# Transposing the first block of x with the DMA crossbar instead of TensorE in a fused two-layer MLP

## The chip, the cores and the metric

The kernel runs on one core of one Trainium2 chip. Times are device microseconds (us) of one execution; medians come from three to eleven executions. A profiled execution has a span, from the first to the last instruction of the program, some 1.8 us shorter than its time (292.11 us had a span of 290.3).

## The reference, cut to what matters

```python
B, S, D, F = 1, 2048, 576, 4608          # x [S, D], w1 [D, F], w2 [F, D], all bf16
h = jnp.einsum("bsd,df->bsf", x, w1) + b1
r = jnp.where(h > zero, h, zero)
h = r * r
out = jnp.einsum("bsf,fd->bsd", h, w2) + b2
```

## The kernel before: the parts that matter

x is worked off in four blocks of 512 rows. The first layer needs x transposed (D on partitions). Blocks 1 to 3 are transposed by the DMA crossbar (`dma_start_transpose`); block 0, which the first matmuls wait for, by TensorE through PSUM. D is 4.5 times 128: four full K tiles (`O` to `O+3`) and a strip. `w1n` holds the first 512 columns of w1 in natural K tiles of 128 ("full matmuls", L194); the other 4,096 columns are in `w1_h`, half of them on partitions 0 to 63 and half on 64 to 127, and are worked off by pairs of 64-row matmuls that run side by side ("row-tiled matmuls", 16 row groups j of 18 matmuls). `w1_h` comes in chunk pairs of one or two row groups: (0,1), (1,2), (2,4) and so on.

```python
WARM = [512] * 6 + [256]
for i, n in enumerate(WARM):             # warm-up of TensorE on constants
    keep(nc.tensor.matmul(wps[:, 0:n], lhsT=ones[:, 0:P], rhs=ones[:, 0:n], start=True, stop=True))
...
load_x(nc.sync, 0); load_x(nc.scalar, 1); load_x(nc.sync, 2); load_x(nc.scalar, 3)   # four lines
for k in range(NK):
    load_w1n(nc.sync, k)
...
for j in range(RT):                      # block 0: 20 TensorE transposes
    ...
    for i in range(3):
        keep(nc.tensor.transpose(ta[:, i, :], xs[:, j, i * P:(i + 1) * P], ident[:]))
    keep(nc.vector.tensor_copy(out=xT0[:, O:O + 3, cols], in_=ta[:, :, :]))
    ...
dup_windows(0)                           # two DVE copies, lower half to upper and back
...
for (j0, j1) in [(0, 1), (1, 2), (2, 4), (4, 6), (6, 8), (8, 10), (10, 12)]:
    load_w1(nc.sync, 0, j0, j1)
    load_w1(nc.sync, 1, j0, j1)
load_xT(1)                               # crossbar transposes of block 1
for (j0, j1) in [(12, 14), (14, 16)]:
    load_w1(nc.sync, 0, j0, j1)
    load_w1(nc.sync, 1, j0, j1)
...
a_full(0, "k_outer")                     # 16 full matmuls, 4 for the strip
a_rows(0, 12, 1)                         # row-tiled matmuls; copies of block 1 at row group 12
```

## Time and profile before

| | |
|---|---|
| time, median of the first three runs | 292.98 us |
| span of the profiled run | 290.3 us |
| TensorE busy | 285.7 us, 98% |
| first full matmul | 5.71 us |
| first row-tiled matmul | 9.75 us |
| w1 pair of row groups 12 and 13 complete | 31.13 us, first used at 33.08 |
| first second-layer matmul | 75.90 us |

The page of the kernel before, its lines of busy time and of the chain that ended last (shares by engine):

```profile
PE 285.7 (98%) x2409; PEld 178.0 (61%) x2412; DVE 81.5 (28%) x189; ACT 94.2 (32%) x154; POOL 2.7 (1%) x10
...
PE 98%; ACT 0%; issue 0%; DVE 0%
```

TensorE does everything, and whatever does not make it wait costs nothing. Its waits, in total over the run (who waited for what: us, times, longest):

```profile
PE wps L61 <- PEq L306: 0.8, 1, 0.8
PE pn L194 <- ACT xTw L143: 0.4, 1, 0.4
PE pn L194 <- issue: 0.3, 2, 0.2
```

So there is 0.4 us to be had from waiting, and the time before the first full matmul. TensorE's timeline in the head (start us, us, engine, line, operation, tiles; in brackets the idle time before it and what ended that):

```profile
0.78 2.93 PE L61 MATMUL wps<-const-bfloat16-1.0 128*128 128x512 bf16 x7 [0.78 <-PEq L306]
...
5.71 1.89 PE L194 MATMUL pn<-xTw,w1n 128*128 128x512 bf16 x8 [0.43 <-ACT xTw L143]
...
9.75 0.38 PE L173 MATMUL ph<-xTw,w_h 64*128 64x512 bf16 x1
```

Warm-up to 3.7 us, transposes between, full matmuls from 5.71, row-tiled ones from 9.75. The SP queue in the same run (the time is from the first issue of a group to the end of the last):

```profile
0.74 0.85 SPq L70 DMA_DIRECT2D x_sb<-in_x_dram  x2
1.65 1.85 SPq L73 DMA_DIRECT2D w1n<-in_w_dram  x4
3.61 13.67 SPq L80 DMA_DIRECT2D w_h<-in_w_dram  x14
17.32 6.75 SPq L120 DMA_TRANSPOSE xTw<-in_x_dram  x1
```

w1 is issued from 3.61 us on, and then the DMA engines have a backlog. The second half of the pair for row groups 12 and 13, looked at alone (its issue on SP, and its time to landing):

```profile
L80 SPq DMA_DIRECT2D w_h<-in_w_dram x1: 638/638/638, 26.1 to 26.1; - x1
...
DMA to landing us min/median/max: 5.1/5.1/5.1
```

It lands at 31.13 us. Row group 12 starts at 33.06 us and needs it at 33.08: **1.95 us to spare**.

### The profile page before, as it was taken

What the parts mean: (1) busy time and instruction counts of PE and PEld (TensorE: products, weight loads), DVE (VectorE), ACT (ScalarE), POOL (GpSimd) and SP (SyncE); (2) the same over time, 40 slices, a digit from 0 to 9 for tenths busy, and PEclk for the clock granted to TensorE, in tenths of its full rate; (3) what the DMA queues carried; (4) which work ended last, traced back from release to release, by engine and by line L of the source; (5) the groups of instructions that cost most, each with busy time, mean ns of one, the idle gap of its engine ahead of it and who ended that gap; (6) DMA issues with size and microseconds to landing.
All of it is one profiled execution on the core that took longest, in us unless ns stands there. A gap on an engine that the chain in (4) does not pass through costs nothing.

```text
span 290.3 us, 5455 instructions
## 1 busy us (share of the span) xinstructions
PE 285.7 (98%) x2409; PEld 178.0 (61%) x2412; DVE 81.5 (28%) x189; ACT 94.2 (32%) x154; POOL 2.7 (1%) x10
## 2 busy tenths in 40 slices
PE   8999999999999999999999999999999999999995
PEld 4444444444677777777744444444447777777774
DVE  3344544444531011110025444444440111100111
ACT  4566666666400000000027666666670000000000
POOL 3000000000000000000000000000000000000000
PEclk9999999999999999999999999999999999999999
DMA  7999999900000000000000000000000000000000
GB/s 203 214 212 177 255 357 265 164 1 2 0 23 0 23 20 20 23 3 20 20 23 0 3 0 2 0 2 0 2 0 2 20 24 20 21 2 23 20 20 24
DMA packets 27096, 16.05 MB, mean 55 GB/s; under 512 B 11028, under 2 KB 27040, under 8 KB 27072
## 3 DMA queue, kind: packets, MB, share of 16 engines
q1 hardware_dynamic: 26688, 15.32, 23.9%
q8 instruction: 19, 0.31, 0.4%
q10 hardware_dynamic: 288, 0.30, 0.3%
q0 software_dynamic: 96, 0.07, 0.1%
q14 instruction: 5, 0.04, 0.0%
HBM read 11.36 MB, written 2.36 MB: 47 GB/s over the span
## 4 chain that ended last, share of the span: by engine, by line
PE 98%; ACT 0%; issue 0%; DVE 0%
PE po L233 49%; PE ph L173 42%; PE pn L194 5%; PE wps L61 1%; PE ph L175 1%; PE pn L188 1%; PE ta L138 0%; ACT xTw L143 0%; DVE o_sb L242 0%; ACT xTw L144 0%; PE tb L141 0%; PE tb L142 0%; PE b1T_ps L151 0%; PE pn L190 0%
## 5 line engine op out<-in xcount | busy, mean ns | idle before, releaser
L233 PE MATMUL po<-w_sb,hT 128*128 128x288 bf16 x1152 | 141.4, 286 | 0.0
L233 PEld LDWEIGHTS <-hT 128*128 128x128 bf16 x1152 | 112.7, 98 | 28.8
L173 PE MATMUL ph<-xTw,w_h 64*128 64x512 bf16 x576 | 124.6, 376 | 0.0
L175 PE MATMUL ph<-xTw,w_h 64*128 64x512 bf16 x576 | 124.6, 376 | 0.0
L173 PEld LDWEIGHTS <-w_h 64*128 64x128 bf16 x576 | 54.1, 94 | 68.3
L161 ACT ACTIVATE r<-ph,b1T 128x512 bf16<-128x512 f32 x128 | 81.1, 685 | 41.6 <-PE ph L175 41.6
L162 DVE TENSOR_TENSOR hT<-r 128x512 bf16<-128x512 bf16 x144 | 61.2, 426 | 77.3 <-ACT r L161 76.7
L175 PEld LDWEIGHTS <-w_h 64*128 64x128 bf16 x576 | 54.1, 94 | 0.0
L242 DVE TENSOR_TENSOR o_sb<-po,b_bc 128x288 bf16<-128x288 f32 x32 | 13.3, 453 | 123.9 <-PE po L233 123.9
L161 ACT ACTIVATE r<-pn,b1T 128x512 bf16<-128x512 f32 x16 | 10.3, 688 | 78.8 <-PE pn L190 77.5
L194 PE MATMUL pn<-xTw,w1n 128*128 128x512 bf16 x61 | 14.0, 379 | 0.8 <-ACT xTw L143 0.4
L194 PEld LDWEIGHTS <-w1n 128*128 128x128 bf16 x64 | 6.0, 98 | 8.0 <-issue 1.4
L61 PE MATMUL wps<-const-bfloat16-1.0 128*128 128x512 bf16 (+1 forms) x7 | 2.9, 594 | 0.8 <-PEq L306 0.8
L113 DVE COPY xTw<-xTw 64x2048 bf16<-64x2048 bf16 x4 | 2.8, 690 | 0.4 <-ACT xTw L144 0.3
L114 DVE COPY xTw<-xTw 64x2048 bf16<-64x2048 bf16 x4 | 2.7, 687 | 0.1
L139 DVE COPY xTw<-ta 128x384 bf16<-128x384 bf16 x4 | 1.3, 358 | 4.2 <-PE ta L138 4.2
L188 PE MATMUL pn<-xTw,w1n_89 64*128 64x512 bf16 x8 | 2.4, 379 | 0.0
L190 PE MATMUL pn<-xTw,w1n_89 64*128 64x512 bf16 x8 | 2.4, 379 | 0.0
L61 PEld LDWEIGHTS <-const-bfloat16-1.0 128*128 128x128 bf16 x7 | 0.9, 135 | 2.1 <-issue 2.1
L98 ACT ACT_TABLE_LOAD x1 | 1.3, 1283 | 1.7 <-PEq L306 1.7
L138 PE MATMUL ta<-ident,x_sb 128*128 128x128 bf16 x12 | 1.6, 265 | 0.0
L143 ACT COPY xTw<-tb 128x128 bf16<-128x128 bf16 x4 | 1.1, 282 | 1.2 <-PE tb L142 1.1
(21 smaller groups left out, 10.2 us busy)
## 6 DMA issues: line engine op xcount, KB each, us to landing
w_sb<-in_w_dram SPq DMA_DIRECT2D x6, 864.0 KB, 11.4
w_h<-in_w_dram SPq DMA_DIRECT2D x14, 288.0 KB, 7.4
out_dram<-o_sb SPq DMA_DIRECT2D x15, 144.0 KB, 1.8
w_h<-in_w_dram SPq DMA_DIRECT2D x4, 144.0 KB, 4.1
w1n<-in_w_dram SPq DMA_DIRECT2D x4, 128.0 KB, 4.0
x_sb<-in_x_dram ACTq DMA_DIRECT2D x2, 144.0 KB, 3.0
x_sb<-in_x_dram SPq DMA_DIRECT2D x2, 144.0 KB, 2.8
b_bc<-in_b_dram SPq DMA_DIRECT2D x1, 144.0 KB, 7.6
```

Source lines behind the costliest of these rows:

```text
L61: keep(nc.tensor.matmul(wps[:, 0:n], lhsT=ones[:, 0:P], rhs=ones[:, 0:n], start=True, stop=True))
L113: keep(nc.vector.tensor_copy(out=xT[0:H, SPC:SPC + 4, :], in_=xT[H:P, E3:E3 + 4, :]))
L114: keep(nc.vector.tensor_copy(out=xT[H:P, SPC:SPC + 4, :], in_=xT[0:H, O:O + 4, :]))
L161: keep(nc.scalar.activation(out=r[:], in_=bank[:], func=ACT.Relu, bias=b1T[:, ft:ft + 1], scale=1.0))
L162: keep(nc.vector.tensor_tensor(out=hTs[sb][:, ft, :], in0=r[:], in1=r[:], op=ALU.mult))
L173: keep(nc.tensor.matmul(bx[:], lhsT=w1_h[0:H, LO_C[i], jc], rhs=xT[0:H, LO_W[i], :], start=(i == 0), stop=(i == NC - 1)))
L175: keep(nc.tensor.matmul(by[:], lhsT=w1_h[H:P, UP_C[i], jc], rhs=xT[H:P, UP_W[i], :], start=(i == 0), stop=(i == NC - 1)))
L188: keep(nc.tensor.matmul(banks[2 * i][:], lhsT=w1n8[0:H, i, :], rhs=xT[0:H, SPC, :], start=start, stop=stop))
L190: keep(nc.tensor.matmul(banks[2 * i + 1][:], lhsT=w1n8[H:P, i, :], rhs=xT[H:P, E3, :], start=start, stop=stop))
L194: keep(nc.tensor.matmul(banks[g][:], lhsT=w1n[:, k, g * P:(g + 1) * P], rhs=xT[:, O + k, :], start=start, stop=stop))
L233: keep(nc.tensor.matmul(po[h][:, 0:DH], lhsT=hT[:, ft, jj * P:(jj + 1) * P], rhs=w2_sb[:, ft, h * DH:(h + 1) * DH], start=(i == 0), stop=( ...
L242: keep(nc.vector.tensor_tensor(out=o_sb[:, h * DH:(h + 1) * DH], in0=po[h][:, 0:DH], in1=b2_bc[:, h * DH:(h + 1) * DH], op=ALU.add,))
```

## The change

The intent: free TensorE of 20 transposes and ACT and DVE of 12 evictions, and start the full matmuls on the first 256 rows while the second 256 are still on their way. The w1n loads move to the ScalarE queue, so that they need not queue behind the transposes.

```diff
-    WARM = [512] * 6 + [256]
+    WARM = [512] * 8
...
-    load_x(nc.sync, 0)
-    load_x(nc.scalar, 1)
-    load_x(nc.sync, 2)
-    load_x(nc.scalar, 3)
+    for h in range(2):
+        rc = slice(h * SB // 2, (h + 1) * SB // 2)
+        keep(nc.sync.dma_start_transpose(out=xT_blk[0][:, O:O + NK, rc], in_=x2[rc, 0:P * NK]))
+    keep(nc.sync.dma_start_transpose(out=xT_blk[0][:, E3:E3 + 1, :], in_=x2[0:SB, D - P:D]))
     for k in range(NK):
-        load_w1n(nc.sync, k)
+        load_w1n(nc.scalar, k)
+    load_w1(nc.scalar, 0, 0, 1)
+    load_w1(nc.scalar, 1, 0, 1)
...   (the TensorE transposes of block 0 and their evictions go)
-                for k in range(NK):
-                    for g in range(G):
-                        full(g, k, k == 0, False)
+                for h in range(2):
+                    hc = slice(h * SB // 2, (h + 1) * SB // 2)
+                    for k in range(NK):
+                        for g in range(G):
+                            keep(nc.tensor.matmul(banks[g][:, hc], lhsT=w1n[:, k, g * P:(g + 1) * P],
+                                                  rhs=xT[:, O + k, hc], start=(h == 0 and k == 0), stop=False, ...))
...
-    for (j0, j1) in [(0, 1), (1, 2), (2, 4), (4, 6), (6, 8), (8, 10), (10, 12)]:
+    for (j0, j1) in [(1, 2), (2, 4), (4, 6), (6, 8), (8, 10), (10, 12)]:
```

More of the change, by code (lines that the diff above doesn't have):

```diff
@@ L58 @@
     ones = nc.const_aps.tensor(1.0, [P, 512], BF16)
-    WARM = [512] * 6 + [256]
+    WARM = [512] * 8
     for i, n in enumerate(WARM):
         keep(nc.tensor.matmul(wps[:, 0:n], lhsT=ones[:, 0:P], rhs=ones[:, 0:n], start=True, stop=True))
-    xs = const.tile([P, RT, D], BF16, name="x_sb")
     w1n = wpool.tile([P, NK, GW], BF16, name="w1n")
@@ L67 @@
     w1_v = w1.rearrange("(c p) f -> p c f", p=H)
-    def load_x(eng, rt):
-        keep(eng.dma_start(out=xs[:, rt, :], in_=x2[rt * P:(rt + 1) * P, :]))
     def load_w1n(eng, k):
@@ L81, in load_w1, with alloc_xT @@
                       in_=w1_v[:, :, GW + h * FH + j0 * P:GW + h * FH + j1 * P]))
-    load_x(nc.sync, 0)
-    load_x(nc.scalar, 1)
-    load_x(nc.sync, 2)
-    load_x(nc.scalar, 3)
+    E3, O, SPC, E = 0, 1, 5, 6
+    xT_blk = {}
+    def alloc_xT(sb):
+        xT_blk[sb] = xtpool.tile([P, NC, SB], BF16, name="xTw", tag="xTw")
+    alloc_xT(0)
+    for h in range(2):
+        rc = slice(h * SB // 2, (h + 1) * SB // 2)
+        keep(nc.sync.dma_start_transpose(out=xT_blk[0][:, O:O + NK, rc], in_=x2[rc, 0:P * NK]))
+    keep(nc.sync.dma_start_transpose(out=xT_blk[0][:, E3:E3 + 1, :], in_=x2[0:SB, D - P:D]))
     for k in range(NK):
-        load_w1n(nc.sync, k)
+        load_w1n(nc.scalar, k)
+    load_w1(nc.scalar, 0, 0, 1)
+    load_w1(nc.scalar, 1, 0, 1)
     ident = const.tile([P, P], BF16, name="ident")
@@ L98 @@
     keep(nc.scalar.activation(out=warm[:], in_=nc.const_aps.tensor(0.0, [P, 1], FP32), func=ACT.Relu))
-    E3, O, SPC, E = 0, 1, 5, 6
     LO_W = [O, O + 1, O + 2, O + 3, E, E + 1, E + 2, E3, SPC]
@@ L104 @@
     UP_C = [1, 3, 5, 7, 8, 2, 4, 6, 0]
-    xT_blk = {}
-    def alloc_xT(sb):
-        xT_blk[sb] = xtpool.tile([P, NC, SB], BF16, name="xTw", tag="xTw")
     def dup_windows(sb):
@@ L130 @@
     b2_bc = const.tile([P, D], BF16, name="b2_bc")
-    alloc_xT(0)
-    xT0 = xT_blk[0]
-    for j in range(RT):
-        cols = slice(j * P, (j + 1) * P)
-        ta = ps_h.tile([P, 3, P], BF16, name="ta", tag="ph")
-        for i in range(3):
-            keep(nc.tensor.transpose(ta[:, i, :], xs[:, j, i * P:(i + 1) * P], ident[:]))
-        keep(nc.vector.tensor_copy(out=xT0[:, O:O + 3, cols], in_=ta[:, :, :]))
-        tb = ps_o.tile([P, 2, P], BF16, name="tb", tag="po")
-        keep(nc.tensor.transpose(tb[:, 0, :], xs[:, j, 3 * P:4 * P], ident[:]))
-        keep(nc.tensor.transpose(tb[:, 1, :], xs[:, j, D - P:D], ident[:]))
-        keep(nc.scalar.copy(out=xT0[:, O + 3, cols], in_=tb[:, 0, :]))
-        keep(nc.scalar.copy(out=xT0[:, E3, cols], in_=tb[:, 1, :]))
     dup_windows(0)
@@ L188, in pair @@
             keep(nc.tensor.matmul(banks[2 * i][:], lhsT=w1n8[0:H, i, :], rhs=xT[0:H, SPC, :],
-                             start=start, stop=stop))
+                             start=start, stop=stop, skip_group_check=order == "k_outer"))
             keep(nc.tensor.matmul(banks[2 * i + 1][:], lhsT=w1n8[H:P, i, :], rhs=xT[H:P, E3, :],
-                             start=start, stop=stop))
+                             start=start, stop=stop, skip_group_check=order == "k_outer"))
         def full(g, k, start, stop):
@@ L205, in a_full @@
             if order == "k_outer":
-                for k in range(NK):
-                    for g in range(G):
-                        full(g, k, k == 0, False)
-                    if k == 1:
-                        make_b1T()
+                for h in range(2):
[3 more added lines that the diff above has]
+                            keep(nc.tensor.matmul(banks[g][:, hc], lhsT=w1n[:, k, g * P:(g + 1) * P],
+                                                  rhs=xT[:, O + k, hc], start=(h == 0 and k == 0), stop=False,
+                                                  skip_group_check=True))
+                        if h == 1 and k == 0:
+                            make_b1T()
             else:
```

## The prediction

> **What bounds the kernel.** TensorE. The chain of waits puts 98% of the 290.3 us span on PE. By stage windows PE is busy 65.1 of 65.25 us (9.75 to 75) and 71.95 of 72.0 (75 to 147); the change touches none of that. Only the head can move. In the timeline warm-up matmuls run 0.78 to 3.71 us, block 0's PE transposes 3.5 to 5.3, the first real matmul starts at 5.71, the row-tiled matmuls at 9.75.
>
> **What it removes.** 20 PE transposes and 12 evictions (DVE 358 ns, ACT about 280 ns). On PE's chain they cost 2.0 us (3.71 to 5.71), but w1n loads meanwhile (lands at 4.9 to 7.3 us), so 1 to 1.5 us at most is on offer.
>
> **What it adds.**
> - Three crossbar transposes on SP. The unobstructed 512x512 one of the trace (issued at 52.5 us) took 2.22 us on SP and 6.6 us to landing; the 512x128 ones 1.25 us on SP, 3.0 to 4.6 us to landing. Estimate for a 256-row half alone: 1.2 us to the first packet, 2 us of packets, 1.4 us to the semaphore, so landing at 5.3 us.
> - Contention. The w1n loads and the first w1 pair (0.8 MB) run on the ScalarE queue beside the transposes. The Trainium skill (DMA: Bandwidth & Descriptors, "Queues, rings and completion order") says that DMA engines take queues in turn, packet by packet (no trace here shows this mix); 1 KB packets beside 256 B ones would take most of the rate until about 5 us. Estimates: first half lands at 6.2 (5.3 to 7.3), second at 7.4, last strip at 8.
> - PE: 32 matmuls of 256 columns for 16 of 512, the same array time (16 x 0.216 = 3.46 us), unless weight loads (98 ns) stop hiding behind 110 ns matmuls: up to 0.3 us. The warm-up ends at 4.2 us instead of 3.7.
>
> **On the critical path.** First real matmul at 6.2 instead of 5.71; 3.6 us of full matmuls to 9.8; the pairs need the strip and one window copy (8 + 0.69): no extra wait. Row-tiled matmuls start at about 10.4 instead of 9.75: +0.65 us. Later w1 chunks: the last two pairs landed 2.0 and 1.4 us ahead of use (31.1 for 33.1, 35.5 for 37). The transposes delay that queue by an estimated 1 to 2 us, PE is itself 0.65 late: 0 to 0.5 us of stall. Sum: +0.8 us.
>
> **Prediction: 293.8 us, range 292.4 to 296.2.** Faster by over 2%: 0.005; within 2%: 0.975; slower by over 2%: 0.02.
>
> **What shows each step.** Timeline: first full matmul between 5.5 and 7.3 us; PE idle about 2 us after the warm-up, released by the transpose's DMA, not by w1n; 32 matmuls about 110 ns apart; row-tiled start 9.9 to 11.5; landings as above; later stage windows unchanged but for small waits on w1 before 38 us.
>
> **What would make it wrong.** (a) The first half lands before 4.7: a gain of up to 1 us. (b) Contention doubles the transposes' time: +2 to 3 us. (c) The idle gap closes the clock gate. The skill (TensorE: Matmul & The Clock Gate, Part 1) gives a window of 3.4 us (here matmuls went from 427 to 216 ns at about 4.5 us, which fits). A 2 us gap should be survived; if not, add 1.5 to 2 us. (d) w1 chunks slip beyond their slack: +1 to 2 us around 33 to 38 us.

## More of the kernel before

One execution was abnormal: the profiled run of the kernel called dead_L took 1,734 us, with TensorE six times as slow as ever (one row group of matmuls took 11.9 us where 1.94 is usual). It is left out of all times. Only its early DMA records are used, and that is said where it is done.

## The result, and the profile after

The median went from 292.80 us (4 runs, 292.60 to 293.26) to 296.52 us (4 runs, 296.03 to 296.91). The ratio is 1.0124, 95% interval 1.0103 to 1.0144. All ratios in this text are the mean time of one kernel's fast runs over that of the other's fast runs of the same rounds, so not quite the ratio of the medians quoted. Slower by 1.2% counts as "the same" at 2%, but it is far outside the noise, and outside the predicted range (292.4 to 296.2). The profiled run of before (292.11 us) is faster than each of its four, and that of after (296.91) is the slowest of its four, so the spans differ by 4.8 us.

The same lines of the page after; the chain now holds DMA and SP:

```profile
PE 286.8 (97%) x2409; PEld 178.0 (60%) x2409; DVE 80.2 (27%) x185; ACT 92.5 (31%) x146; POOL 2.7 (1%) x10
...
PE 86%; SPq 8%; DMA 4%; issue 0%; DVE 0%
```

TensorE's waits after. There are now three kinds of data to wait for, x, w1n and w1:

```profile
PE pn L196 <- DMA xTw<-in_x_dram: 1.8, 2, 1.0
PE pn L196 <- DMA w1n<-in_w_dram: 1.1, 1, 1.1
PE ph L161 <- DMA w_h<-in_w_dram: 1.1, 1, 1.1
PE wps L61 <- PEq L296: 0.8, 1, 0.8
```

TensorE's timeline in the head, after:

```profile
0.78 3.57 PE L61 MATMUL wps<-const-bfloat16-1.0 128*128 128x512 bf16 x8 [0.78 <-PEq L296]
5.36 1.71 PE L196 MATMUL pn<-xTw,w1n 128*128 128x256 bf16 x12 [1.01 <-DMA xTw<-in_x_dram]
8.17 0.61 PE L196 MATMUL pn<-xTw,w1n 128*128 128x256 bf16 x4 [1.09 <-DMA w1n<-in_w_dram]
9.61 0.60 PE L196 MATMUL pn<-xTw,w1n 128*128 128x256 bf16 x4 [0.82 <-DMA xTw<-in_x_dram]
...
11.94 0.38 PE L159 MATMUL ph<-xTw,w_h 64*128 64x512 bf16 x1
```

The first full matmul comes 0.35 us *earlier* than before. Then the last w1n tile is waited for until 8.17 us and the second row half until 9.61, and the row-tiled matmuls start at 11.94 us, 2.19 us late. Two short waits for the first and the third w1 pair follow, seen at TensorE's weight loads (PEld):

```profile
12.44 0.09 PEld L161 LDWEIGHTS <-w_h 64*128 64x128 bf16 x1 [0.61 <-DMA w_h<-in_w_dram]
16.59 0.09 PEld L161 LDWEIGHTS <-w_h 64*128 64x128 bf16 x1 [0.58 <-DMA w_h<-in_w_dram]
```

With them TensorE is 2.96 us late from row group 3 on (by the start of the second of each pair of matmuls). The crossbar transposes of block 0 on SP (ns on SP, min/median/max, and the time from issue to landing):

```profile
L88 SPq DMA_TRANSPOSE xTw<-in_x_dram x2: 1286/1304/1322, 0.7 to 2.1; - x2
L89 SPq DMA_TRANSPOSE xTw<-in_x_dram x1: 1254/1254/1254, 3.5 to 3.5; - x1
...
DMA to landing us min/median/max: 4.6/7.1/7.4
```

The first half took 4.6 us (landed at 5.32), as estimated for one alone. The second took 7.4 (9.56 us) and the strip 7.1 (10.61). The next place where time goes is at row group 12, in TensorE's timeline:

```profile
36.11 0.39 PE L159 MATMUL ph<-xTw,w_h 64*128 64x512 bf16 x1
37.58 0.39 PE L161 MATMUL ph<-xTw,w_h 64*128 64x512 bf16 x1 [1.08 <-DMA w_h<-in_w_dram]
```

The pair of row groups 12 and 13, complete at 31.13 us before, is complete at 37.53 now: its second half was issued late and then took no longer than before:

```profile
L76 SPq DMA_DIRECT2D w_h<-in_w_dram x1: 634/634/634, 32.7 to 32.7; - x1
...
DMA to landing us min/median/max: 4.8/4.8/4.8
```

From 40 us on nothing differs (TensorE is busy 35.00 of the 35 us from 40 to 75), and the first second-layer matmul starts at 80.42 us instead of 75.90: +4.52 us.

### The profile page after: what moved, and what is told of

The parts are those of the page before. It is cut to its first block, busy times and chain, and to the rows that moved or that the text cites. A ratio compares the mean times of both kernels' runs of the same rounds, so it can differ in the third digit from the quotient of the medians.

```text
span 295.1 us, 5438 instructions
## 1 busy us (share of the span) xinstructions
PE 286.8 (97%) x2409; PEld 178.0 (60%) x2409; DVE 80.2 (27%) x185; ACT 92.5 (31%) x146; POOL 2.7 (1%) x10
## 4 chain that ended last, share of the span: by engine, by line
PE 86%; SPq 8%; DMA 4%; issue 0%; DVE 0%
PE po L223 48%; PE ph L159 21%; PE ph L161 13%; SPq L76 5%; PE pn L180 4%; SPq L119 3%; DMA xTw<-in_x_dram 3%; DMA w_h<-in_w_dram 2%; SPq L88 0%; SPq L120 0%; PE pn L174 0%; DVE o_sb L232 0%; PE pn L176 0%
## 5 line engine op out<-in xcount | busy, mean ns | idle before, releaser
L180 PE MATMUL pn<-xTw,w1n 128*128 128x512 bf16 x48 | 10.9, 379 | 0.0
L180 PEld LDWEIGHTS <-w1n 128*128 128x128 bf16 x48 | 4.5, 98 | 5.9 <-issue 0.8
L196 PE MATMUL pn<-xTw,w1n 128*128 128x256 bf16 x32 | 4.2, 273 | 3.0 <-DMA xTw<-in_x_dram 1.8
L196 PEld LDWEIGHTS <-w1n 128*128 128x128 bf16 x32 | 3.0, 99 | 4.8 <-issue 2.8
L61 PE MATMUL wps<-const-bfloat16-1.0 128*128 128x512 bf16 x8 | 3.6, 628 | 0.8 <-PEq L296 0.8
L73 POOL DMA_DIRECT2D w1n_89<-in_w_dram x2 | 1.2, 629 | 0.0
```

What stands on the lines that cost most here:

```text
L180: keep(nc.tensor.matmul(banks[g][:], lhsT=w1n[:, k, g * P:(g + 1) * P], rhs=xT[:, O + k, :], start=start, stop=stop))
L196: keep(nc.tensor.matmul(banks[g][:, hc], lhsT=w1n[:, k, g * P:(g + 1) * P], rhs=xT[:, O + k, hc], start=(h == 0 and k == 0), stop=False, s ...
```

## The experiments

Fourteen kernels ran; all gave correct results. Theory A, to begin with: the transposes make the whole early DMA stream late, above all w1. Its rivals: B, only the late head counts; C, SP is held back by waits for completions; D, the halves and 256-column matmuls cost; E, the second queue costs by itself. Theories on the clock (H), on a drain per transpose (P) and on DMA engines in step (L) came up on the way.

### The queue change alone (q_only)

```diff
 # against before
-    load_x(nc.scalar, 1)            # and row tile 3 likewise
+    load_x(nc.sync, 1)
-        load_w1n(nc.sync, k)
+        load_w1n(nc.scalar, k)
```

> Kernel before with the queue part alone: all four x loads on SP, the four w1n loads on the ScalarE queue, TensorE transposes kept, no crossbar transpose of block 0. Theory A (the crossbar transposes beside the w1n loads move too few bytes per us, so the whole w1 stream comes late): no loss, 0.998 to 1.003 of before, first w1 chunks landing within 1 us of before's (8.5 and 9.95 us), packets of 256 B about 20 ns. Rival E (two hardware queues at once are what slows the start): at least +1.5 us and packets of w1 slow (over 28 ns) here too.

Measured: 296.33 us, ratio 1.0117, against 292.37 for before: as slow as the whole change, and not what I expected. In the profiled run (293.86 us) w1 was on time (first chunk at 7.84 us, 7.75 before), so neither A nor E as I had put it holds. The loss there is in the head: with w1n on its own queue its bytes arrive beside x and not behind it, and with all of x on SP the last x load is issued at 2.13 us and not at 1.18 (the edit does both). The last x tile landed at 6.50 us (4.36 before), and the first full matmul came at 7.43 us. The three timed runs were another 2.3 to 2.9 us slower (296.18 to 296.79), and they have a mean granted TensorE clock of 0.994 where the profiled run has 1.0: 0.6% of 294 us is 1.7 us lost, one stretch of 3.4 us at half clock (the profile of w1n_pairs, below, has such a stretch). So there was a third cause to look at, the clock gate; it covers 1.7 of the 2.3 to 2.9 us.

### Filling the gaps of that kernel (q_warm)

```diff
 # against q_only
+        if j >= 1:
+            for _ in range(3):
+                keep(nc.tensor.matmul(wps[:, 0:512], lhsT=ones[:, 0:P], rhs=ones[:, 0:512], start=True, stop=True))
         ta = ps_h.tile([P, 3, P], BF16, name="ta", tag="ph")
```

> q_only with three more 512-column warm-up matmuls ahead of each of the last three row tiles' transposes, which fill TensorE's waits for x. In three of four runs of q_only the mean granted clock was 0.994 (1.7 us lost) at 294.3 to 295.0 us of span, in the fourth 1.0 at 292.1. Theory H (the gaps of 0.4 to 0.6 us in the head make the clock gate close once more for one window): all four runs at 0.998 to 1.0, median 293 to 294.5. Rival E (the two queues are slow by themselves, the clock is a bystander): the median stays near 296.

Measured: 294.44 us, ratio 1.0066, clock 0.999 to 1.0 in all four runs. Theory H holds: with the gaps filled by useless matmuls the gate stayed open and 1.9 us came back. What stays over before (1.8 us) is the late x: first row-tiled matmul at 11.70 us, +1.94. For the kernel after itself the gate is not the cause as far as its profile shows: the clock opened at 4.33 us, as early as in before (4.52), and stayed open until TensorE was done, and this run was the slowest of the four. The mean clock of its other runs (0.998 to 1.0) says less: the profiles of one_queue and w1_first have a mean of 1.0 too, though their clock opened only at 12.18 and 9.18 us. The records begin at the first opening, so 0.994 points to a later closing (what closed at the end of a profiled run cost 0.002 at most), but 1.0 does not show an early opening.

### Transposes that nobody reads (dead_T), and plain loads that nobody reads (dead_L)

```diff
 # against before, behind the w1n loads on SP
+    dead = const.tile([P, 5, SB], BF16, name="dead")
+    for h in range(2):
+        rc = slice(h * SB // 2, (h + 1) * SB // 2)
+        keep(nc.sync.dma_start_transpose(out=dead[:, 1:1 + NK, rc], in_=x2[rc, 0:P * NK]))
+    keep(nc.sync.dma_start_transpose(out=dead[:, 0:1, :], in_=x2[0:SB, D - P:D]))
 # dead_L instead:
+    dead = const.tile([P, RT, D], BF16, name="dead")
+    for rt in range(RT):
+        keep(nc.sync.dma_start(out=dead[:, rt, :], in_=x2[rt * P:(rt + 1) * P, :]))
```

> Kernel before plus the same three crossbar transposes into a tile that nobody reads, on SP behind the w1n loads; TensorE's own head is untouched, so the first full matmul stays near 5.7 us and the first row-tiled one near 9.8 to 10.5. Theory A: the w1 stream comes 3 us or more late and TensorE stalls on w1 before 40 us: +1.5 to +4 us though no matmul reads the transposes. Rival B (only the wait of the head for the transposes costs): within 0.7 us of before.

> Kernel before plus four plain loads of block 0 of x (576 KB) into a tile nobody reads, at the place where dead_T had its three transposes. Theory A with the transposes as the cause: the plain loads delay the w1 stream by only 1.6 to 2.2 us (dead_T: 3.7 us at the first chunk and 4.6 at the third pair), so +0 to +1.2 us in time against +3.9 for dead_T. Rival (any extra 0.6 MB at that place costs this): +3 us or more.

Measured: dead_T 296.28 us, ratio 1.0127; dead_L 293.71 us (its three normal runs), ratio 1.0041 (interval 1.0024 to 1.0058). TensorE's waits in dead_T:

```profile
PE ph L180 <- DMA w_h<-in_w_dram: 1.2, 2, 0.9
PE ph L178 <- DMA w_h<-in_w_dram: 1.0, 1, 1.0
```

No matmul reads these transposes, and yet they cost 3.7 us by the ratio, nearly all of it at waits on w1, and all of it before row group 4: from there on TensorE is 3.80 us late, and row group 12 adds nothing. (The first full matmul is 0.46 us later, but so is that of before_w1, whose head is that of before. In these two profiles the clock opened at 6.46 and 5.87 us, and in before at 4.52: a single profile's head can differ by this much.) This is against rival B and for theory A, that w1 comes late. The same data as plain loads costs 1.2 us. In the landings, the third w1 pair's first half came at 11.34 us before, 13.62 with the plain loads (from the abnormal execution's DMA records, where w1 does not depend on TensorE) and 15.93 with the transposes. So at that place the three transposes delay the stream by 4.6 us, the plain loads by 2.3.

A rival: that SP takes long to issue transposes. The SP queue in dead_T, and then in dead_L (early records of the abnormal execution):

```profile
3.64 3.02 SPq L92 DMA_TRANSPOSE dead<-in_x_dram  x2
6.71 1.26 SPq L93 DMA_TRANSPOSE dead<-in_x_dram  x1
8.01 13.98 SPq L80 DMA_DIRECT2D w_h<-in_w_dram  x14
```

```profile
3.68 1.75 SPq L91 DMA_DIRECT2D dead<-in_x_dram  x4
5.48 14.58 SPq L80 DMA_DIRECT2D w_h<-in_w_dram  x14
```

The first w1 load is issued 4.40 us later than in before (3.61 us) and 1.87 us later: nearly all of the 4.6 and most of the 2.3. Meanwhile the DMA engines ran short of work in dead_T (from 9 to 10 us; the last two figures are their busy share and GB/s):

```profile
9.00:10.00 1.00, 1.00 (x7) 0.34 (x7) 0.00 (x0) 0.00 (x0) 0.00 (x0) 1.00 0.29 67
```

So what dead_T shows is the time that transposes take on SP. In the kernel after it is another matter: there SP issued its first w1 load (of the second pair) at 4.76 us, not later than in before (5.05), and the DMA engines were busier and moved less. From 2 to 13 us in before, then in after:

```profile
2.00:13.00 11.00, 10.57 (x78) 5.31 (x78) 4.82 (x12) 5.95 (x16) 1.38 (x3) 1.00 1.08 244
2.00:13.00 11.00, 7.88 (x50) 4.19 (x50) 1.57 (x3) 2.02 (x3) 1.39 (x3) 1.00 1.27 180
```

This agrees with theory A as it stands in q_only's expectation (too few bytes per us), but no experiment isolates it.

### Everything on one queue (one_queue), with a longer warm-up (one_queue_warm), with one transpose (one_queue_ns)

```diff
 # one_queue, against after
+    for k in range(NK):
+        load_w1n(nc.sync, k)            # ahead of the transposes
     for h in range(2):
         ...
-    for k in range(NK):
-        load_w1n(nc.scalar, k)
-    load_w1(nc.scalar, 0, 0, 1)         # the first w1 pair goes back to SP too
-    load_w1(nc.scalar, 1, 0, 1)
 # one_queue_warm, against one_queue
-    WARM = [512] * 8
+    WARM = [512] * 16
 # one_queue_ns: one_queue with one 512-row transpose and 512-column matmuls
```

> Kernel after with everything of the head on SP, w1n first, then the three transposes, then w1. Theory A with mixing as the cause: the transposes, now with no other hardware queue beside them, land within 4.5 us of their issue each (after: 3.2, 7.4 and 7.2 us), w1 packets stay near 20 ns and 47 ns, loss under 2 us. If instead the transposes slow the DMA engines by themselves: w1 chunks late by 3 us or more as in after, loss 3 to 4 us, one queue or two.

> one_queue with 16 warm-up matmuls in place of 8, which fill TensorE's wait until the first half lands at 7.0 us. Theory H (in the profile of one_queue the clock opened at 12.2 us only, and three timed runs have 0.994, because the wait of 2.7 us falls into the gate's window): the clock opens before 8 us and stays open, no run at 0.994, time 1.2 to 2.6 us less than one_queue, 292.8 to 294.2. Rival (the clock is a bystander): within 0.5 us of one_queue.

> one_queue with a single 512-row transpose (and 512-column matmuls) in place of the two halves. Theory P (each transpose has a drain of about 1 us in which the DMA engines move little, so a third transpose instruction costs the stream about 1 us): the transposes' last strip and the first w1 chunk land 0.6 to 1.2 us earlier than in one_queue (8.6 and 9.9 us), time 0.5 to 1.5 us less than one_queue. Rival D (the 256-column matmuls are what costs): strip and w1 chunk land as in one_queue, within 0.3 us, and only matmul times change.

Measured: one_queue 295.36 us (ratio 1.0105), one_queue_warm 294.98 (1.0080), one_queue_ns 297.97 (1.0178). In one_queue the three transposes landed 4.4, 4.1 and 3.2 us after their issue (7.4 and 7.1 for the last two in after), which points to the traffic beside them as what stretched them in after (their order and time of issue changed as well). But the loss is 3.1 us by the ratio, not under 2 as expected: they are issued later here, so is w1 (first load at 6.78 us, behind the transposes on SP, and not at 3.61), the first matmul starts at 7.06 us, and its wait of 2.71 us went with a clock gate that stayed shut: by the clock records of the trace it opened at 12.18 us only. The three timed runs (0.994) point to a closing after the opening. With 16 warm-up matmuls the clock opened at 4.66 us, no run was below 1.0, and the row-tiled matmuls started at 11.14 us instead of 13.63. That is 2.5 us won in the head; the time fell by only 0.4 us (0.7 by the ratios), because TensorE now waited for w1 (0.97 us at 16 us) and row groups 12 and 13 were late as well. The single transpose, expected to win about 1 us, took 6.4 us to land and lost 2.6 (part of it to the clock: three timed runs have 0.988 or 0.994): theory P falls, at least as I had put it.

### The halves (no_split), and the same with a longer warm-up (no_split_warm)

```diff
 # no_split, against after
-    for h in range(2):
-        rc = slice(h * SB // 2, (h + 1) * SB // 2)
-        keep(nc.sync.dma_start_transpose(out=xT_blk[0][:, O:O + NK, rc], in_=x2[rc, 0:P * NK]))
+    keep(nc.sync.dma_start_transpose(out=xT_blk[0][:, O:O + NK, :], in_=x2[0:SB, 0:P * NK]))
     ...  (and the 512-column matmuls of before)
 # no_split_warm, against no_split
-    WARM = [512] * 8
+    WARM = [512] * 16
```

> Kernel after without the row halves: one 512-row transpose and matmuls of 512 columns. Theory A: the w1 stream is as late as in after (chunk of rows 12 and 13 lands at 36 to 38 us), so the total is within 0.7 us of after although the first full matmul starts later (8 to 10 us instead of 5.4). Rival D (the halves and the 256-column matmuls cost the time): faster than after by 1 us or more. Rival B (the late start of the head alone sets the loss): slower than after by 1 us or more, as the first matmul starts later.

> no_split with 16 warm-up matmuls in place of 8, which fill the wait until the 512 rows land at 6.7 us. Theory H: the first 8 full matmuls take 1.9 us and not 3.2 as in no_split, the row-tiled start comes 0.8 to 1.4 us earlier (10.7 to 11.3 us), time 0.8 to 1.6 us less than no_split, unless the w1 stream now ends the stall (chunk of rows 12 and 13 landed at 34.6 us there, with 0.9 us to spare). Rival: within 0.4 us of no_split.

Measured: no_split 294.93 us, ratio 1.0092; no_split_warm 295.18 us, ratio 1.0090. By the ratios no_split is 0.9 us better than after, between what A and D had expected, and the intervals overlap; D is not settled by the time. The traces show that 256-column matmuls are not what costs (in after, twelve of them took 1.47 us), but all 512 rows together landed at 6.68 us here, and in after the second half alone at 9.56. In one_queue it was the other way round. Whether halves help depends on what runs beside them, and I can't say how.

The pair shows better than any other how a gain is given back. TensorE's first full matmuls in no_split, and then in no_split_warm:

```profile
6.73 3.23 PE L178 MATMUL pn<-xTw,w1n 128*128 128x512 bf16 x8 [2.37 <-DMA xTw<-in_x_dram]
```

```profile
6.74 1.89 PE L178 MATMUL pn<-xTw,w1n 128*128 128x512 bf16 x8
```

The longer warm-up did what it should: the clock is open, eight matmuls take 1.89 us and not 3.23, and the row-tiled start comes 1.0 us earlier (11.13 us). Yet the time is the same. TensorE's waits in no_split_warm show where it went:

```profile
PE ph L159 <- DMA w_h<-in_w_dram: 0.8, 1, 0.8
```

This wait is at 35.7 us, row group 12 again. In no_split no matmul waited for w1.

### Where w1 is issued from (w1_sp, w1n_pairs), and in which order (w1_first)

```diff
 # w1_sp, against after: the first w1 pair back on SP, behind the transposes
-    load_w1(nc.scalar, 0, 0, 1)
-    load_w1(nc.scalar, 1, 0, 1)
 # w1n_pairs, against after: two w1n loads of 256 KB
-    for k in range(NK):
-        load_w1n(nc.scalar, k)
+    for k in (0, 2):
+        keep(nc.scalar.dma_start(out=w1n[:, k:k + 2, :],
+                                 in_=w1[k * P:(k + 2) * P, 0:GW].rearrange("(k p) f -> p k f", p=P)))
 # w1_first, against after: the last two w1 pairs ahead of block 1's transposes
-    for (j0, j1) in [(1, 2), (2, 4), (4, 6), (6, 8), (8, 10), (10, 12)]:
+    for (j0, j1) in [(1, 2), (2, 4), (4, 6), (6, 8), (8, 10), (10, 12), (12, 14), (14, 16)]:
```

> Kernel after with the first w1 pair on SP behind the transposes, so that only w1n is on the ScalarE queue. In after and in the run without halves the 512 B packets of w1 took 54 ns and their completions came in groups of 16, in the other runs 47 ns and spread out. Theory L (a w1 pair issued from two queues beside transposes puts the 16 DMA engines in step): 47 ns here, w1 stream 1 us or more earlier by 25 us than in after. Rival (w1n on the ScalarE queue beside the transposes does it): 54 ns here as well. In time I expect 0 to 1.5 us less than after.

> Kernel after with w1n in two loads of 256 KB in place of four of 128 KB. SP then has two transfers fewer ahead of the one that has to wait for the second half's completion, so more w1 chunks are issued before it is held (6.5 to 9.6 us in after). Rival C (SP held by that completion makes the w1 stream late): w1 chunks from the third pair on land 1.5 to 3 us earlier and the time falls by 1 us or more. Theory A (the DMA engines, not SP's issue, are the limit): third pair within 0.7 us of after's 15.0 and 16.5 us, time within 0.7 us of after.

> Kernel after with the last two w1 chunk pairs (rows 12 to 15) loaded ahead of the crossbar transposes of block 1 instead of behind them. Theory A (two lateness terms, of the head, 2.2 us up to the first row-tiled matmul plus 0.8 us of small waits on w1 before 20 us, and of the w1 stream, 1.3 us at 36 us): the wait on w1 at 36 us disappears, the head stays as it is, so 0.7 to 1.5 us faster than after and still 2 to 3.3 us slower than before. Rival B (the head alone): no change against after, within 0.4 us.

Measured: w1_sp 296.56 us (1.0137), w1n_pairs 296.52 (1.0137), w1_first 296.22 (1.0116): all within noise of after.

w1_sp was to test theory L, on why w1 comes more slowly in after. It falls: with only w1n on the ScalarE queue the 512-byte packets still took 53 ns (54 in after and 47 in before, means from 13.5 to 21.5 us). DMA rates from 13.5 to 21.5 us, when nothing but w1 is loaded, in before, after and one_queue_warm (the last figure of a row is GB/s):

```profile
13.50:21.50 8.00, 8.00 (x78) 3.62 (x76) 3.68 (x9) 5.07 (x8) 0.00 (x0) 1.00 1.23 212
```

```profile
13.50:21.50 8.00, 7.91 (x74) 3.42 (x72) 4.24 (x11) 6.09 (x11) 0.00 (x0) 1.00 1.23 187
```

```profile
13.50:21.50 8.00, 7.03 (x65) 3.03 (x63) 3.40 (x8) 4.97 (x9) 0.00 (x0) 1.00 1.23 191
```

All kernels with transposes beside ScalarE loads have 187 to 195 GB/s long after both are done; all others have 202 to 214, but for one: one_queue_warm, with one queue, has 191. So the w1 loads have a faster and a slower mode, and what sets it is **open**.

w1n_pairs was to test rival C. In after SP could not issue from 6.5 to 9.6 us, as its next transfer had to wait for the second half's completion. Here that hold is 0.6 us, and the third pair came 1.2 us earlier, between what C (1.5 to 3) and A (at most 0.7) had said; in w1_sp, with a hold of 0.7 us, it came 0.7 us earlier. The time fell in neither. In the profiled run of w1n_pairs the wait for the first half (3.18 us) went with a clock that closed again for 3.4 us, so the head was later (row-tiled start 12.75 us); but this run is the fastest of its four, so why the others did not gain is not shown. C may account for up to a third of the 3.65 us by which the third pair is late in after, and is not ruled out for that part.

w1_first removed the wait at 36 us, as it should, and was expected to win 0.7 to 1.5 us. It won 0.3 us, if anything: in its profiled run the clock opened at 9.18 us only, and the first w1 pair's second half, on the ScalarE queue, was waited for at 13.2 us (0.96 us). This miss and no_split_warm's pointed to one rule.

### The rule, and its test (ns_warm_w1, with the control before_w1)

Theory M: two streams run side by side, the head of TensorE's work and w1, and they meet at row group 12. What comes after is shifted by the *larger* of two terms, not by their sum: the shift of the first row-tiled matmul, and the lateness of the w1 pair of row groups 12 and 13 minus the 1.95 us it had to spare. From the profiled runs, in us:

| kernel | head shift | w1 pair late by | minus 1.95 | larger | measured shift of second layer |
|---|---|---|---|---|---|
| after | 2.19 | 6.40 | 4.45 | 4.45 | 4.52 |
| w1_sp | 1.60 | 5.57 | 3.62 | 3.62 | 3.69 |
| dead_T | 1.79 | 5.57 | 3.62 | 3.62 | 3.80 |
| one_queue_warm | 1.39 | 4.88 | 2.93 | 2.93 | 3.00 |
| no_split_warm | 1.38 | 4.51 | 2.56 | 2.56 | 2.63 |
| w1n_pairs | 3.00 | 4.90 | 2.95 | 3.00 | 3.02 |
| no_split | 2.37 | 3.45 | 1.50 | 2.37 | 2.37 |
| one_queue | 3.88 | 2.83 | 0.88 | 3.88 | 3.87 |
| one_queue_ns | 5.12 | 3.94 | 1.99 | 5.12 | 5.12 |
| q_only | 1.72 | 0.05 | none | 1.72 | 1.72 |
| q_warm | 1.94 | 2.85 | 0.90 | 1.94 | 1.94 |
| w1_first | 2.13 | 2.13 | 0.18 | 2.13 | 3.47 (plus the wait at 13.2 us) |

The table has limits. It is read against one profile of before, a fast run, so its shifts are some tenths larger than those between medians. And the head shift stops at the first row-tiled matmul, while waits for the first w1 pairs come after it. Just before row group 12 the shift was 2.96 us in after, 2.21 in w1_sp, 3.80 in dead_T, 2.74 in one_queue_warm, 1.67 in no_split_warm and 3.47 in w1_first. So in dead_T the whole loss was there before row group 12, and that 3.62 comes near it is chance; w1_first is no exception but shows the same third term. With the shift just before row group 12 in place of the head, all twelve rows agree within 0.1 us. In this form the rule is little more than bookkeeping: TensorE goes on when both it and the pair are ready. It says where time is lost, and not why w1 is late.

The rule was made from these runs, so it had to predict a new one: take the w1 term of row group 12 away, and leave a head that the longer warm-up has shortened.

```diff
 # ns_warm_w1, against no_split_warm; before_w1 is the same edit to before
-    ... (8, 10), (10, 12)]:
+    ... (8, 10), (10, 12), (12, 14), (14, 16)]:          # load_xT(1) now comes behind them
-    a_rows(0, 12, 1)
+    a_rows(0, 14, 1)
```

> no_split_warm (one transpose, 16 warm-up matmuls) with the last two w1 pairs loaded ahead of block 1's crossbar transposes, and block 1's window copies two row groups later. Theory M (the shift of everything after 40 us is the larger of two terms: the shift of the first row-tiled matmul, and the lateness of the w1 pair of rows 12 and 13 minus the 1.95 us it had to spare in the kernel before; no_split_warm: 1.4 and 2.6, measured 2.6): with the w1 term taken away only the head is left, first second-layer matmul 1.3 to 1.8 us later than before's 75.9, time 1.3 to 1.9 us over before. Rival (the two terms are a story, something else costs 2.5 us): time stays 2.3 to 2.9 us over before.

> Control: the kernel before with the same reordering of w1 and of block 1's window copies and nothing else. In before no matmul waits for that w1 pair, so theory M gives no change, within 0.4 us of before. If the order by itself gains 0.5 us or more, the gain of ns_warm_w1 does not show what theory M says.

Measured over five rounds: ns_warm_w1 293.82 us, ratio 1.0047 (interval 1.0033 to 1.0060), against 292.49 for before: 1.3 us over it, where the rival said 2.3 or more. before_w1 292.51 us, ratio 0.9999 (0.9986 to 1.0012): the order by itself gives nothing. In the profile of ns_warm_w1 the only wait of a matmul in the view is the start of the program; two weight loads still waited for an early w1 pair:

```profile
PE wps L61 <- PEq L287: 0.8, 1, 0.8
PEld L159 <- DMA w_h<-in_w_dram: 0.6, 2, 0.4
```

Its second layer started 1.15 us late and its row-tiled matmuls 0.86 us. The time lies in the stated range (1.3 to 1.9 over before), the shift a little below the stated 1.3 to 1.8, as the head was better in this run. This is the best version with the crossbar, and it still loses to before: no version that beats both was found.

## Why the prediction was wrong, point by point

- **Direction and place: right.** A loss was predicted, in the head and in late w1 chunks before 38 us, and nothing later changed.
- **First full matmul: better than predicted.** 5.36 us against 6.2; the first half landed at 5.32, as estimated for one alone.
- **Second half and strip: wrong.** Predicted to land at 7.4 and 8 us, they landed at 9.56 and 10.61, and TensorE also waited for w1n until 8.17 us, which was said not to happen. one_queue points to the traffic beside them as what stretched them: there each landed 3.2 to 4.4 us after its issue. The contention was seen as a risk, (b) in the text, but only the first half was given its worst case. The head is 2.19 us late instead of 0.65.
- **The step that failed most:** "The transposes delay that queue by an estimated 1 to 2 us, PE is itself 0.65 late: 0 to 0.5 us of stall." The pair of row groups 12 and 13 was 6.40 us late, and TensorE's shift grew by 2.3 us between the first row-tiled matmul and the second layer (2.19 to 4.52): 0.8 at the first three w1 pairs, for which the prediction had no figure, and 1.6 at row group 12 (risk (d)). Of the 6.40 us, 3.65 were there at the third pair. They built up while the DMA engines were busy but moved 180 GB/s instead of 244 (2 to 13 us), and while SP was held for 3.1 us; what each is worth is not separated. The 4.6 us of dead_T are no measure of it, as they are mostly time on SP. 1.8 came between the third and the seventh pair, of which 0.8 up to 22.8 us, while w1 alone was loading, at 187 instead of 212 GB/s, and the rest partly beside block 1's first transpose. 0.9 came at the end, behind block 1's transposes. Why the rates were lower stays open.
- **The sum: right in form, wrong in its terms.** The stall was worked out net of the head's lateness ("PE is itself 0.65 late"), and the head plus such a stall is the larger of the two terms of the table. For after, the w1 term (4.45) is the whole shift and the head's 2.19 us are hidden in it.
- **256-column matmuls: right.** Twelve in 1.47 us.
- **The clock gate, risk (c): right for the profiled run.** TensorE's gap after the warm-up was 1.01 us, not 2, and the clock opened at 4.33 us and stayed open. Six sibling kernels had runs in which the gate opened late or closed again, at a cost of 1.3 to 2.5 us where it was measured.

## What to carry to other kernels

A unit that is nearly always busy hides how little slack the streams behind it have: before a change adds bytes or slow transfers to the front of a queue, look up how many microseconds early the *last* loads of that queue land, not only the first, and how long its engine takes to issue what is added (three transposes took 4.4 us of SP in dead_T). When two late things feed one engine, their costs combine as a maximum, so repairing one may show nothing until the other is repaired as well; test them together, with a control. And moving loads to a second queue changes which bytes arrive first, and a gap of a few microseconds in TensorE's warm-up may cost more than the work that was removed.

## What the Trainium skill lacked or had wrong

- Advanced Engine Details and Errata, "X-Bar Transpose (TRN2)": "TRN2 transpose DMAs are as fast as regular DMAs". The section has no figure for the time on the issuing engine, and that was the larger part here: in dead_T a half took SP 1.33 to 1.64 us and the strip 1.26, a plain load of 128 rows in dead_L 0.33 to 0.43. Three transposes (640 KB) had w1 issued 4.40 us later and the run lose 3.7 us, plain loads of the same rows (576 KB) 1.87 and 1.2 us. For the transfer itself these runs do not contradict the page: from issue to landing a half (256 KB) took 4.3 us, a plain load (144 KB) 3.7 to 4.0.
- DMA: Bandwidth & Descriptors, "Issuing engines are not separate DMA queues", says that issuing from several engines "will only save the time on the sequencer". It also changes what lands first: with w1n on ScalarE's queue beside all of x on SP's, the last x tile landed at 6.50 us instead of 4.36 (0.95 us of this is its later issue). The page does say that queues interleave, and q_only agrees: x tiles landed at 3.54, 4.17, 5.46 and 6.50 us, w1n tiles at 3.71, 4.39, 6.20 and 6.82.
- TensorE: Matmul & The Clock Gate, "Why this matters for your kernels", asks for no TensorE gaps above some 3 us. In q_only, whose profiled run had gaps of 0.4 to 0.6 us in the head (the timed runs have no trace of theirs), three of four runs show 1.7 us lost to the clock; with a gap of 2.71 us in one_queue the clock opened at 12.2 us. In one_queue_warm, whose warm-up lasts nearly until the data is there, it opened at 4.66. Its window of 3.4 us (Part 1) fits: in w1n_pairs the clock closed for 3.41 us.
- No page: the same w1 loads ran at 202 to 214 or at 187 to 195 GB/s from 13.5 to 21.5 us, with nothing else being loaded. What sets the mode is open.
- No page: a crossbar transpose of the same 512 rows landed 5.4 to 6.4 us after its issue in four kernels, and a half of them 4.1 to 8.1 in others, which differed in what ran beside it.
